# Sliding-window attention gated by a SiLU feed-forward layer: where Wo's halves are stored, how early raw weights are fetched, and where the last transposes stand

## The chip, the cores and the metric

The kernel runs on one core of one Trainium2 chip. The core has a matrix engine (TensorE, "PE" in the profile, with its weight loads as "PEld"), three engines for elementwise work (VectorE "DVE", ScalarE "ACT", GpSimd "POOL"), a queue engine (SyncE, "SP") and 16 DMA engines. Each engine works through its own list of instructions in order and waits on semaphores for the others. The metric is the time of one execution in device microseconds; lower is better.

## The reference

All arrays are float32; x is 2048 x 640 (S x D). With xn = layernorm(x), without learned scale:

```
q, k, v = split(xn @ wqkv) into 32 heads of 20
logits[s, w] = q[s] . k[s - 2 w] / sqrt(20)       w = 0..7, positions below 0 masked
o[s] = sum over w of softmax(logits[s])[w] * v[s - 2 w]
s_out = o @ wo                                      wo: 640 x 640
h = silu(xn @ w1);  g = silu(h @ w2)                w1: 640 x 1536, w2: 1536 x 640
out = x + s_out * g
```

## The kernel before, in words

**Precision.** PE multiplies in a float32 format of reduced precision (fp32r). To keep float32's, each operand is split in two halves: the high half is a rounded copy, the low half what is left. A product takes three passes: high x high, low x high, high x low. For a weight chunk the split is one ACT copy (L407) and one subtraction (L413, on DVE but for the first few). A chunk that has been split once can be kept in DRAM as a pair of halves (`half_...`, stored by L418) and loaded back by POOL's queue in one transfer (L399) with no work on ACT or DVE. A pair has 640 KB, the raw chunk 320 KB.

**Groups and stages.** The 2048 positions are worked on in four groups of 512: two halves of the sequence, each cut into even and odd positions, so that the window of stride 2 has stride 1 inside a group. In a group, `qkv_phase` computes q, k and v in four quarters of the heads, each from five weight chunks; evacuations go to ACT, and `halo` copies the seven earlier rows that a window needs from one partition to the next (L509 on SP). `scores` and `values` do the attention on DVE, in broadcast multiplies and reductions; this is long and runs behind the matmuls, into the next stage. `ffn_phase` then does, for f = 0 to 12, the first product of w1 chunk f (15 matmuls of 512 columns, L888 to L890) and the second product of w2 chunk f - 1 (12 pairs of 384 and 256 columns, L743 and L745).

**Wo, one group late.** The attention output of group g is transposed and split during the q/k/v stage of group g + 1 (`o_chunk`, through L475), and its product with Wo (`wo_phase`, five chunks of 12 pairs, L743/L745 again) stands in `ffn_phase` of group g + 1 behind the first product of f = 0. So Wo is used four times: in groups 1, 2 and 3, and at the end (`wo_last`) for group 3's own output. Group 3's output is transposed inside group 3's feed-forward stage, the last two chunks of it by `o_rest` (L590). `wo_rest` finishes group 2's rows there: four adds on DVE (L804) and four stores of output rows (L806).

**Units.** The list `units` names every use of a weight chunk in order of use: 44 in group 0 (20 of q/k/v, 24 of w1 and w2), 49 in each later group, 5 at the end. In group 1 the Wo chunks are units 65 to 69, in group 2 114 to 118, in group 3 163 to 167, at the end 191 to 195. Unit i lives in slot i mod 7 of the ring `WR`; `w_load` is called for the next unit when one has been used (`w_done`), so a load can run seven units ahead. `what` says how each use gets its halves: "split" (raw load, split, nothing kept), "store" (raw load, split, halves kept in DRAM), "load" (halves from DRAM). `store_at` is the use at which the halves are stored: the first one, but the second for the q/k/v chunks with odd c.

**Raw chunks.** The raw chunks (`fresh` lists their units) are fetched by SP (`raw_load`, L379/L381) into buffers: in group 0 into several tiles, later into the two tiles `XR` in turn. The fetch of the chunk two further on in `fresh` is asked for at each split. `XR` also takes the rows of x that `wo_phase` adds to the result (L788, the add on POOL L789, the store L791).

**The order of the work.** Nothing is issued as the program text runs. Each operation is added to `Weave` with an engine, a modelled duration, what it reads and writes, and a priority. `Weave.order` then plays the program through with these durations (a DMA model of one shared pipe of 310 KB per us plus a landing time of 1.9 us) and always starts the operation that can start first, the lower priority number among those ready. PE's operations keep the order in which they were added. The order so found is emitted, each engine's list in order; on the chip the engines keep it even where the real times differ from the modelled ones. ACT's weight copies have the lowest priority, raw loads on SP `clock + 5`, halo copies `clock`, stores of halves `due + 25`.

Of the kernel before, what the change touches and what calls it, by code (L numbers as in the profile page):

```python
# [15 lines left out]
S, D, F, H, DH = 2048, 640, 1536, 32, 20  # L16
W = 8
DC, FC = D // P, F // P
# [9 lines left out]
EPS = 1e-5  # L28
CA, CB = 384, 256
RING = 7  # L30
WARM, WARM2 = 20, 3
HOLD = 3.4
LO = 10
# [142 lines left out]
def local_attention_silu_ffn(ctx: ExitStack, tc: tile.TileContext, x, wqkv, wo, w1, w2, out):  # L176
# [126 lines left out]

    def store_at(u):

        return 1 + (u[0] == "q" and u[2] % 2)

    first_q = NQ * DC

# [27 lines left out]
    def raw_load(k):  # L337
# [43 lines left out]
                nc.sync.dma_start(to, by)  # L381
        dma(go, [], kr, n * P * 4, 1 + k if k < 2 * DC else clock[0] + 5, (0.62 if k < 2 * DC else 0.45) * (1 + len(more)))

    def w_load():
        i = loaded[0]
        if i >= len(units):
            return
        loaded[0] += 1
        u, s = units[i], i % RING
        n = width(i)  # L390
        r = WR[s]
        at = start(i)
        both = r.rearrange("p (s d) -> p s d", s=2)[:, :, at:at + n]
        whi, wlo = both[:, 0], both[:, 1]
        kh, kl = ("wh", s), ("wl", s)
        due = clock[0]
        if what[i] == "load":
            src = halves[u]
            add("POOL", 1.0, lambda: nc.gpsimd.dma_start(both, src), [("half", u), ("half", u, "more")], [kh, kl], due + 10,  # L399
                nbytes=2 * n * P * 4)  # L400
            return
        k = fresh.index(i)
        if not k:
            raw_load(0)
            rawn[0] = 1
        raw, kr = raws.pop(i)
        act(n, lambda: nc.scalar.activation(whi, raw, AF.Copy), kr + [("sd", 0)] * (k < 2), [kh], 1000 + due)  # L407
        pool_does = k < LO and k not in ON_DVE
        eng, cost, by = ("POOL", po(n), nc.gpsimd) if pool_does else ("DVE", dv(n), nc.vector)
        parts = HALVES if pool_does and k < DC else 1  # L410
        for j in range(parts):
            cs = slice(j * n // parts, (j + 1) * n // parts)
            add(eng, po(n // parts) if pool_does else cost, lambda cs=cs: by.tensor_tensor(  # L413
                out=wlo[:, cs], in0=raw[:, cs], in1=whi[:, cs].bitcast(F32), op=OP.subtract), [kh] + kr,
                [kl if j == parts - 1 else kl + (j,)], due if pool_does else LOW_AT if k < LO else 50, lock=True)
        if what[i] == "store":
            def keep(to, a, b, key):
                dma(lambda: nc.sync.dma_start(to, both[:, :, a:b].bitcast(F32)), [kh, kl], [key], 2 * (b - a) * P * 4,  # L418
                    due + 25)
            wide = width(len(units) - 1 - units[::-1].index(u))  # L420
            kept = dram.tile([P, 2, wide], F32, name="half_" + "_".join(map(str, u)))
            halves[u] = kept
            past = n - wide if u[0] == "q" and u[1] == NQ - 1 else 0
            keep(kept[:, :, :n - past], past, n, ("half", u))
            for k in range(past // MORE):
                v = ("q", k, u[2])
                keep(halves[v][:, :, 3 * CQ:], k * MORE, (k + 1) * MORE, ("half", v, "more"))
        while rawn[0] <= (min(k + 6, early - 1) if k < early - 2 else k + 2):
            raw_load(rawn[0])
            rawn[0] += 1  # L430

    def w_next(*want):

# [322 lines left out]
    def gkeys(ts, cs):  # L756
        return [("g", t, cs.start) for t in range(ts.start, ts.stop)]
# [34 lines left out]

    rest = []

    def wo_rest(g):

        done = [("o", NQ - 1, t) for t in (0, 2)]
        for t, xr, kx in rest:
            if t >= 2:
                dma(lambda t=t, xr=xr: nc.sync.dma_start(xr, rows(xg, g)[:, t, :]), done, [(kx[0], t)] if t > 2 else kx,  # L800
                    P * D * 4, clock[0])
        for t, xr, kx in rest:
            kx = [(kx[0], t)] if t > 2 else kx
            dve(D, lambda t=t, xr=xr: nc.vector.tensor_tensor(out=xr, in0=xr, in1=G[:, t, :], op=OP.add),  # L804
                done + gkeys(slice(t, t + 1), slice(0, CA)) + gkeys(slice(t, t + 1), slice(CA, D)), kx, 600, lock=True)
            dma(lambda t=t, xr=xr: nc.sync.dma_start(rows(og, g)[:, t, :], xr), kx, [], P * D * 4, clock[0] + 5)  # L806

    def wo_last(g, i):
# [52 lines left out]
    def ffn_phase(g, i, ix, io):  # L861
        nxt = g + 1 if g + 1 < NG else None
        ps = prev = None
        for f in range(FC + 1):
            if nxt is not None and f == 0:
                load_x(nxt, 0, 2)
                load_x(nxt, 2, 2)
                for t in range(T):
                    ln_stats(t)
                ln_rstd(0, T)  # L870
                for t in range(T):
                    ln_apply(t)
            if nxt is not None and XT_AT <= f < XT_AT + DC:
                split_t(XIN, [("xin", t) for t in range(T)], f - XT_AT, ix, (TH, TL))
            if nxt is None and f in OL_AT:
                o_chunk(g, OL_AT[f], io)
            if nxt is None and f in REST_AT:
                o_rest(g, REST_AT[f], io)
            cur = None
            if f < FC:  # L880
                wh, wl, kh, kl = w_next("w1", f)
                h, kp = rot()
                s = f % 2

                def first(cs=range(DC), wh=wh, wl=wl, h=h):
                    for c in cs:
                        cs = tsl(c)
                        nc.tensor.matmul(h, wh[:, cs], TH[i][:, c, :], start=c == 0, stop=False)  # L888
                        nc.tensor.matmul(h, wh[:, cs], TL[i][:, c, :], start=False, stop=False)  # L889
                        nc.tensor.matmul(h, wl[:, cs], TH[i][:, c, :], start=False, stop=c == DC - 1)  # L890
                if nxt is None and f == FC - 1:
                    pe(12 * mm(TOK), lambda first=first: first(range(4)), t_keys(i, range(DC)) + [kh, kl], [kp])
                    o_rest(g, (2, 3), io)
                    wo_rest(g - 1)
                    pe(3 * mm(TOK), lambda first=first: first(range(4, DC)), t_keys(i, range(DC)) + [kh, kl], [kp])
                else:
                    pe(15 * mm(TOK), first, t_keys(i, range(DC)) + [kh, kl], [kp])
                w_done()
                sf, sh, sl = SF[s], SH[s], SL[s]
                act(TOK, lambda sh=sh, h=h: nc.scalar.activation(sh, h, AF.Silu), [kp], [("sh", s)], 0, "silu")  # L900
                act(TOK, lambda sf=sf, h=h: nc.scalar.activation(sf, h, AF.Silu), [kp], [("sf", s)], 0, "silu")
                dve(TOK, lambda sf=sf, sh=sh, sl=sl: nc.vector.tensor_tensor(
                    out=sl, in0=sf, in1=sh.bitcast(F32), op=OP.subtract), [("sf", s), ("sh", s)], [("sl", s)], 0, lock=True)
                cur = sh, sl, ("sh", s), ("sl", s)
                if g and f == 0:
                    wo_phase(g - 1, io)
            if f:
                sh, sl, ksh, ksl = prev
                if ps is None:
                    ps = tm_banks()  # L910
                a, b = ps
                wh, wl, kh, kl = w_next("w2", f - 1)
                for t in range(T):
                    def big(t=t, f=f, wh=wh, wl=wl, sh=sh):
                        tm_mm(ps, t, sh[:, tsl(t)], wh, f == 1, False)
                        tm_mm(ps, t, sh[:, tsl(t)], wl, False, False)

                    def small(t=t, f=f, wh=wh, sl=sl):
                        tm_mm(ps, t, sl[:, tsl(t)], wh, False, f == FC)
                    ko = [a[t][1], b[t // 2][1]]  # L920
                    pe(2 * TM, big, [ksh, kh, kl], ko)
                    if f == FC:
                        pe(TM, small, [ksl, kh], ko)
                    else:
                        late.append((TM, small, [ksl, kh], ko))
                for args in late:
                    pe(*args)
                late.clear()
                w_done()
            prev = cur  # L930
        for p, kp, ts, cs in tm_views(ps):
            n = (ts.stop - ts.start) * (cs.stop - cs.start)
            act(n, lambda p=p, ts=ts, cs=cs: nc.scalar.activation(G[:, ts, cs], p, AF.Silu), [kp], gkeys(ts, cs), 0, "silu")
# [41 lines left out]
```

## Time and profile before

| | us |
|---|---|
| median of 3 runs (lowest, highest) | 643.68 (641.07, 643.97) |
| the profiled execution: its own time | 643.34 |
| its span, first to last instruction | 641.5 |
| PE busy | 632.7 |
| DVE busy | 537.5 |
| ACT busy | 210.2 |
| POOL busy | 117.7 |

The mean granted clock of PE was 0.995 of full speed. The DMA queues moved 162.45 MB, 82.58 of them on POOL's queue (q0) and 78.88 on SP's (q1). Group 0 takes about the first 148 us, groups 1, 2 and 3 about 160 us each, and `wo_last` the last 18 or so.

Lines such as "DVE pr L532 <- DMA kv<-kv: 36.8, 2, 30.2" say: DVE, at line 532, which writes pr, waited for the transfer named; 36.8 us in total, twice, 30.2 the longest. In a timeline a row has its start, its duration, the engine, the line, the operation, output and input tiles and their shapes, and in brackets how long the engine was idle before it and what released it.

### The profile page before, as it was taken

Reading aid. Unit: us, or ns where it says so; the run is one execution under the profiler, and the core shown is the slowest. Engines: PE = TensorE matmul, PEld = TensorE weight load, DVE = VectorE, ACT = ScalarE, POOL = GpSimd, SP = SyncE. Lnnn points to the kernel's source line nnn. Section 1 sums busy time; section 2 is a strip of 40 time slices with the busy share of each in tenths; the row PEclk is TensorE's granted clock in tenths of the full one; section 3 lists DMA queues with packets and bytes.
Section 4 is the critical chain, followed back from the end, with each engine's and each line's share of the span. In section 5 each row is a group of like instructions: output and inputs, shape, how many; then the busy total and the mean of one; then the engine's idle time right before and its main releaser. Section 6 shows DMA issues by size and latency. Waiting matters only on the chain.

```text
span 641.5 us, 9077 instructions
## 1 busy us (share of the span) xinstructions
PE 632.7 (99%) x3495; PEld 572.1 (89%) x3495; DVE 537.5 (84%) x543; ACT 210.2 (33%) x439; POOL 117.7 (18%) x164
## 2 busy tenths in 40 slices
PE   7999999999999899999999999999999999999997
PEld 6888899998889898999888999999988999899997
DVE  6699899999989778989959998999504999999824
ACT  4535463443435013142423302323313231223220
POOL 4410000001110134111222115211222211111100
PEclk8999999999999999999999999999999999999999
DMA  9899999877998988756699998855769998566652
GB/s 284 286 305 299 308 385 403 346 217 218 315 281 263 327 298 257 250 173 214 189 257 230 316 261 286 275 179 172 231 174 278 245 315 261 177 196 190 187 198 82
DMA packets 77499, 162.45 MB, mean 253 GB/s; under 512 B 9248, under 2 KB 38912, under 8 KB 77456
## 3 DMA queue, kind: packets, MB, share of 16 engines
q0 software_dynamic: 26672, 82.58, 43.9%
q1 hardware_dynamic: 50240, 78.88, 39.3%
q8 instruction: 27, 0.44, 0.3%
q10 hardware_dynamic: 544, 0.41, 0.2%
q14 instruction: 16, 0.13, 0.1%
HBM read 109.55 MB, written 34.16 MB: 224 GB/s over the span
## 4 chain that ended last, share of the span: by engine, by line
PE 93%; DVE 3%; DMA 2%; issue 1%; ACT 0%; DVEq 0%; ACTq 0%
PE acc L743 21%; PE acc L745 14%; PE acc L709 9%; PE acc L707 9%; PE acc L708 9%; PE rot L890 8%; PE rot L889 8%; PE rot L888 8%; PE rot L475 2%; DMA xr<-in_A_wo_dram 2%; PE acc L650 2%; DVE w L413 1%; DMA xin<-in_A_x_dram 1%; DVE l L535 0%; DVE st L615 0%
## 5 line engine op out<-in xcount | busy, mean ns | idle before, releaser
L532 DVE TENSOR_TENSOR pr<-q,kv 128x2560 f32<-128x2560 f32 x32 | 90.3, 2821 | 36.9 <-DMA kv<-kv 36.8
L743 PE MATMUL acc<-w,sh 128*128 128x384 f32 x384 | 113.6, 335 | 0.0
L707 PE MATMUL acc<-w,th 128*128 128x512 f32 (+2 forms) x300 | 113.3, 378 | 0.0
L709 PE MATMUL acc<-w,th 128*128 128x512 f32 (+2 forms) x300 | 112.9, 376 | 0.0
L708 PE MATMUL acc<-w,tl 128*128 128x512 f32 (+2 forms) x300 | 112.8, 376 | 0.0
L745 PE MATMUL acc<-w,sh 128*128 128x256 f32 x384 | 107.1, 279 | 0.0
L888 PE MATMUL rot<-th,w 128*128 128x512 f32 x240 | 95.8, 399 | 0.0
L890 PE MATMUL rot<-th,w 128*128 128x512 f32 x240 | 94.0, 392 | 0.0
L889 PE MATMUL rot<-tl,w 128*128 128x512 f32 x240 | 93.9, 391 | 0.0
L564 DVE TENSOR_TENSOR pr<-e,kv 128x2560 f32<-128x2560 f32 x32 | 90.3, 2823 | 0.7
L535 DVE TENSOR_REDUCE l<-pr 128x128 f32<-128x2560 f32 x32 | 90.1, 2815 | 0.4
L399 POOL DMA_DIRECT2D w<-half_q x52 | 37.4, 719 | 238.9 <-DVE pr L569 93.2
L569 DVE TENSOR_TENSOR pr<-pr 128x1280 f32<-128x1280 f32 x64 | 76.0, 1188 | 1.0
L399 POOL DMA_DIRECT2D w<-half_w x72 | 38.6, 537 | 198.7 <-PE acc L745 88.7
L745 PEld LDWEIGHTS acc<-w,sh 128*128 128x128 f32 x384 | 72.3, 188 | 1.6
L743 PEld LDWEIGHTS acc<-w,sh 128*128 128x128 f32 x384 | 72.1, 188 | 1.7
L900 ACT ACTIVATE sh<-rot 128x512 fp32r<-128x512 f32 x48 | 28.7, 599 | 126.1 <-PE rot L890 121.4
L709 PEld LDWEIGHTS acc<-w,th 128*128 128x128 f32 x300 | 56.3, 188 | 8.8
L708 PEld LDWEIGHTS acc<-w,tl 128*128 128x128 f32 x300 | 56.3, 188 | 8.6
L707 PEld LDWEIGHTS acc<-w,th 128*128 128x128 f32 x300 | 56.3, 188 | 8.5
L743 PE MATMUL acc<-w,sl 128*128 128x384 f32 x192 | 57.9, 333 | 0.0
L491 ACT ACTIVATE kv<-acc 128x320 f32<-128x320 f32 x64 | 28.3, 442 | 84.8 <-PE acc L709 82.2
(94 smaller groups left out, 1003.7 us busy)
## 6 DMA issues: line engine op xcount, KB each, us to landing
w<-half_w POOLq DMA_DIRECT2D x72, 640.0 KB, 5.3
w<-half_q POOLq DMA_DIRECT2D x39, 512.0 KB, 4.1
half_w<-w SPq DMA_DIRECT2D x24, 640.0 KB
w<-half_wo POOLq DMA_DIRECT2D x15, 640.0 KB, 9.0
kv<-kv SPq DMA_DIRECT2D x16, 560.0 KB
kv<-kv SPq DMA_DIRECT2D x16, 420.0 KB
gate<-in_B_w_dram SPq DMA_DIRECT2D x16, 320.0 KB
w<-half_q POOLq DMA_DIRECT2D x13, 384.0 KB, 4.7
```

The lines of the kernel that those rows point to most:

```text
L399: add("POOL", 1.0, lambda: nc.gpsimd.dma_start(both, src), [("half", u), ("half", u, "more")], [kh, kl], due + 10, nbytes=2 * n * P * 4)
L532: dve(2560, lambda t=t: nc.vector.tensor_tensor(out=PR, in0=win(qq[:, t:t + 2, :], W, 0), in1=win(kv[:, 0, t:t + 2, :], W, CQ), op=OP.mult ...
L535: dve(2560, lambda t=t: nc.vector.tensor_reduce(out=l[:, t:t + 2].rearrange("p t w h -> p (t w h)"), in_=PR.rearrange("p t w (h d) -> p (t ...
L564: dve(2560, lambda t=t, v=v: nc.vector.tensor_tensor(out=PR.rearrange("p t w (h d) -> p t (w h) d", d=DH), in0=e[:, t:t + 2].rearrange("p ...
L707: nc.tensor.matmul(o, hi, wh, start=c == 0, stop=False)
L708: nc.tensor.matmul(o, lo, wh, start=False, stop=False)
L709: nc.tensor.matmul(o, hi, wl, start=False, stop=c == DC - 1)
L743: nc.tensor.matmul(a[t][0][:, :CA], st, w[:, :CA], start=first, stop=last)
L745: nc.tensor.matmul(b[t // 2][0][:, h * CB:(h + 1) * CB], st, w[:, CA:], start=first and h == 0, stop=last, skip_group_check=True)
L888: nc.tensor.matmul(h, wh[:, cs], TH[i][:, c, :], start=c == 0, stop=False)
L889: nc.tensor.matmul(h, wh[:, cs], TL[i][:, c, :], start=False, stop=False)
L890: nc.tensor.matmul(h, wl[:, cs], TH[i][:, c, :], start=False, stop=c == DC - 1)
```

## The change

Three parts.

1. `store_at` gives Wo's chunks 2 instead of 1. Units 65 to 69 are now "split", 114 to 118 "store", the later ones "load" as before.
2. The loop that asks for raw chunks becomes the function `raws_due`, which also runs when a unit is loaded as halves, and stops at a raw chunk whose unit lies more than `RAW_AHEAD` = 10 units ahead of the one now being loaded.
3. In the last group, the first product of f = 11 is cut after the second of its five chunks instead of the fourth; the transposes of `o_rest` and the work of `wo_rest` stand at the cut. The four adds of `wo_rest` also read all tiles of the halves of group 3's attention output, so that they come after the last of these are written.

```diff
+RAW_AHEAD = 10
...
-        return 1 + (u[0] == "q" and u[2] % 2)
+        return 1 + (u[0] == "wo" or u[0] == "q" and u[2] % 2)
...
+    def raws_due(i, k):
+
+        while rawn[0] <= (min(k + 6, early - 1) if k < early - 2 else k + 2):
+            if rawn[0] < len(fresh) and fresh[rawn[0]] > i + RAW_AHEAD:
+                break
+            raw_load(rawn[0])
+            rawn[0] += 1
+
     def w_load():
...
             add("POOL", 1.0, lambda: nc.gpsimd.dma_start(both, src), [("half", u), ("half", u, "more")], [kh, kl], due + 10,
                 nbytes=2 * n * P * 4)
+            raws_due(i, sum(j < i for j in fresh) - 1)
             return
...
-        while rawn[0] <= (min(k + 6, early - 1) if k < early - 2 else k + 2):
-            raw_load(rawn[0])
-            rawn[0] += 1
+        raws_due(i, k)
...
-    def wo_rest(g):
+    def wo_rest(g, i):
...
-                done + gkeys(slice(t, t + 1), slice(0, CA)) + gkeys(slice(t, t + 1), slice(CA, D)), kx, 600, lock=True)
+                done + t_keys(i, range(DC)) + gkeys(slice(t, t + 1), slice(0, CA)) + gkeys(slice(t, t + 1), slice(CA, D)), kx, 600, lock=True)
...
-                    pe(12 * mm(TOK), lambda first=first: first(range(4)), t_keys(i, range(DC)) + [kh, kl], [kp])
+                    pe(6 * mm(TOK), lambda first=first: first(range(2)), t_keys(i, range(DC)) + [kh, kl], [kp])
                     o_rest(g, (2, 3), io)
-                    wo_rest(g - 1)
-                    pe(3 * mm(TOK), lambda first=first: first(range(4, DC)), t_keys(i, range(DC)) + [kh, kl], [kp])
+                    wo_rest(g - 1, io)
+                    pe(9 * mm(TOK), lambda first=first: first(range(2, DC)), t_keys(i, range(DC)) + [kh, kl], [kp])
```

## The prediction

> **What bounds the kernel now.** I read the page first, then the table of waits, then the PE timeline around the waits it names. "Unit 69" is the 70th entry of the list of weight units, and so on.
>
> ```profile
> span 641.5 us, 9077 instructions
> ...
> PE 632.7 (99%) x3495; PEld 572.1 (89%) x3495; DVE 537.5 (84%) x543; ACT 210.2 (33%) x439; POOL 117.7 (18%) x164
> ...
> PE 93%; DVE 3%; DMA 2%; issue 1%; ACT 0%; DVEq 0%; ACTq 0%
> ```
>
> TensorE sets the time: 632.7 of 641.5 us busy. The change removes no matmul, so it can only touch PE's waits, or matmuls that ran slowly while counted as busy. The waits (who waited for whom: total, times, longest):
>
> ```profile
> DVE pr L532 <- DMA kv<-kv: 36.8, 2, 30.2
> ...
> ACT w L407 <- DMA xr<-in_A_wo_dram: 12.9, 1, 12.9
> ...
> PE acc L743 <- ACT w L407: 1.5, 1, 1.5
> ...
> PE acc L743 <- DVE w L413: 0.3, 1, 0.3
> ```
>
> PE waited 1.8 us behind one raw chunk of Wo: its load is late, ACT's copy (the high half) waits 12.9 us for it, the DVE subtraction (the low half) follows, PE last. The real loss is larger. The PE timeline (start, duration) and the stretches around the wait (length; busy per engine; PEclk, DMA share, GB/s):
>
> ```profile
> 213.80 0.33 PE L743 MATMUL acc<-w,th 128*128 128x384 f32 x1
> ...
> 219.25 0.33 PE L743 MATMUL acc<-w,tl 128*128 128x384 f32 x1
> ...
> 226.91 0.40 PE L888 MATMUL rot<-th,w 128*128 128x512 f32 x1
> ```
>
> ```profile
> 219.50:222.00 2.50, 0.76 (x4) 0.30 (x2) 0.84 (x2) 0.74 (x1) 0.00 (x0) 1.00 0.99 380
> ...
> 223.00:226.00 3.00, 3.00 (x13) 3.00 (x13) 3.00 (x4) 0.00 (x0) 0.54 (x2) 0.50 1.04 328
> 226.00:227.00 1.00, 1.00 (x8) 1.00 (x8) 0.72 (x3) 0.00 (x0) 0.61 (x1) 0.98 0.91 287
> ```
>
> From 213.80 to 219.25 there are 19 pairs (a 384- and a 256-column matmul): 5.45 / 19 = 0.287 us a pair. Unit 69, the fifth Wo chunk, would start at 219.25 + 0.287 = 219.54, and its 12 pairs (four token tiles, three passes) would end at 219.54 + 3.44 = 222.98. The next product started at 226.91, so the loss is **3.93 us**: 1.8 of waiting, and 2.15 because the granted clock was 0.50 from 223 to 226. That is 0.6% of the run, and the one place in groups 1 to 3 where PE waits.
>
> **Why the chunk was late.** SP's issues around it, with the copies, the subtractions and the weight load that compete:
>
> ```profile
> 197.56 0.36 SPq L379 DMA_DIRECT2D xr<-in_A_wo_dram  x1
> 198.02 0.37 SPq L418 DMA_DIRECT2D half_wo<-w  x1
> ...
> 198.95 1.27 SPq L418 DMA_DIRECT2D half_wo<-w  x1
> 203.48 4.26 SPq L509 DMA_DIRECT2D kv<-kv  x4
> ...
> 208.31 0.36 SPq L379 DMA_DIRECT2D xr<-in_A_wo_dram  x1
> 208.72 1.57 SPq L418 DMA_DIRECT2D half_wo<-w  x2
> ```
>
> ```profile
> 203.75 1.38 ACT L407 ACTIVATE w<-xr 128x640 fp32r<-128x640 f32 x2
> ...
> 220.38 0.74 ACT L407 ACTIVATE w<-xr 128x640 fp32r<-128x640 f32 x1 [12.85 <-DMA xr<-in_A_wo_dram]
> ```
>
> ```profile
> 204.93 1.55 DVE L413 TENSOR_TENSOR w<-xr,w 128x640 fp32r<-128x640 f32 x2
> ```
>
> ```profile
> 202.35 0.54 POOL L399 DMA_DIRECT2D w<-half_w  x1 [13.46 <-PE acc L709]
> ```
>
> The last raw chunk is issued at 208.31 and used at 220.38, 12.07 us later. In the queues (q1 is SP's, q0 POOL's; packets, MB, share of 16 engines), first 200 to 204 us, then 204 to 214:
>
> ```profile
> q1 hardware_dynamic: 469, 1.66, 102.4%
> ```
>
> ```profile
> q1 hardware_dynamic: 604, 1.31, 53.7%
> q0 software_dynamic: 277, 1.27, 51.5%
> ```
>
> Between 200 and 204, q1 moves 1.66 MB, mainly the two stores, and POOL's load of 202.35 moves nothing. That load then shares 204 to 214 with the halo (the four L509 copies, about 1.1 MB) that stands ahead of the raw chunk. The two stores of 208.72 follow.
>
> **The change, part by part.**
>
> *Stores move from group 1 to group 2.* Five stores of 640 KB (3.28 MB) leave 198 to 222 us. Without the first two the load of 202.35 moves at once: 0.66 MB at 1.66/4 = 0.415 MB/us is 1.6 us, done near 204.5, and the halo then shares q1's time with two loads instead of three. The halo plus chunk (1.1 + 0.33 MB), at the 0.26 MB/us that both queues moved in 204 to 214 with a load of 0.66 MB between, needs 2.1/0.26 = 8 us from 204: landing near 212, latest perhaps 216. PE needs the high half at 219.54, so the load must land by 219.54 - 0.74 = 218.8. I take the whole 3.93 us as gained; bounds 0 and -3.93.
>
> *Group 2 uses raw chunks.* The five POOL loads of the halves go; five raw loads (1.64 MB), five copies, five subtractions and five stores come. The group before:
>
> ```profile
> 350.55 0.54 POOL L399 DMA_DIRECT2D w<-half_wo  x1 [2.15 <-PE acc L709]
> ...
> 361.85 0.53 POOL L399 DMA_DIRECT2D w<-half_w  x1 [1.55 <-PE acc L709]
> ```
>
> ```profile
> 362.98 3.09 SPq L509 DMA_DIRECT2D kv<-kv  x4
> ```
>
> ```profile
> 364.84 0.68 DVE L480 TENSOR_TENSOR tl<-rot,th 128x512 fp32r<-128x512 f32 x1
> ```
>
> ```profile
> 365.26 0.34 PE L743 MATMUL acc<-w,th 128*128 128x384 f32 x1
> ...
> 382.48 0.40 PE L888 MATMUL rot<-th,w 128*128 128x512 f32 x1
> ```
>
> Work: 5 x 0.69 = 3.5 us on ACT (1.38 / 2 each), idle two thirds of the time, and 5 x 0.78 = 3.9 us on DVE (1.55 / 2 each). DVE is late here, but its 30.2 us wait (the row of L532 above, at the start of group 3) takes up such a delay. Without that cover 3.9 us would be the price. SP's ten more issues of about 0.4 us here stand in a queue that is mostly idle; POOL loses five of 0.54. Cost 0.
>
> The wait is the point. Group 2's Wo product starts at 365.26, group 1's at 219.54 - 48 x 0.287 = 205.76: the same pattern 159.5 us later, with the halo at 362.98 (203.48 + 159.5) and the weight load at 361.85 (202.35 + 159.5). So group 2 will have what group 1 had: two raw loads, two stores, halo, fifth raw chunk (unit 118), two stores. What differs is the issue. The chunk's buffer is free when the third chunk's subtraction is done; that fits behind L480 (ends 365.52), so 366.3, and SP's halo issues end at 366.07 (3.09 us here, 4.26 in group 1). Issue near 366.4 is 206.9 on group 1's clock, 1.4 us earlier. With the same 12.07 us it lands at 378.5. PE needs the high half at 365.26 + 48 x 0.287 = 379.04 and gets it at 379.25; it needs the low half one pair later, 379.33, and gets it near 380.05. Wait: 0.2 + 0.5 = **0.7 us**, too short, I judge, to lower the clock. Upper end by the nearest row: the landing hangs on the queue, not the issue, so 220.38 + 159.5 = 379.9, and the loss repeats at 3.93. Lower end 0: 0.7 us less would do, and halo copies that are issued in 3.09 us instead of 4.26 may leave the queue sooner by that much. I take 0.7, nearer to the row of the issue than to that of the landing, since the chunk goes straight behind the halo in both.
>
> The row for the clock: 1.8 us of idling within 2.3 us was followed by 3 us at 0.50. The Trainium skill (TensorE: Matmul & The Clock Gate, Part 1, What's actually happening) has the clock fall after an idle window of about 3.4 us. The trace had it fall after less. By that rule a wait of up to 1.8 us in group 2 would cost the wait alone, and the rival that repeats the loss would give an estimated 641.5; by the row it gives 643.7.
>
> *Raw loads at most ten units ahead.* Units 114 and 115 (Wo in group 2) are asked for when units 104 and 105 are loaded, not already at 68 and 69, where they would hold both XR buffers through group 1's output rows. Group 0 and 1 keep their order, since a raw load there comes at most six units ahead. Cost 0; the cover is the two-buffer ring, idle between the groups.
>
> *Last transposes after the second chunk.*
>
> ```profile
> 610.19 0.39 PE L888 MATMUL rot<-th,w 128*128 128x512 f32 x1
> ...
> 611.56 0.60 PE L590 MATMUL rot<-ident,o 128*128 128x128 f32 x4
> ...
> 612.70 0.34 PE L743 MATMUL acc<-w,sh 128*128 128x384 f32 x1
> ```
>
> ```profile
> 606.89 0.49 DVE L572 TENSOR_TENSOR o<-pr 128x320 f32<-128x320 f32 x1
> ...
> 612.27 1.56 DVE L804 TENSOR_TENSOR pr<-pr,gate 128x640 f32<-128x640 f32 x2 [1.95 <-DMA pr<-in_A_x_dram]
> ...
> 614.35 0.68 DVE L902 TENSOR_TENSOR sl<-sf,sh 128x512 fp32r<-128x512 f32 x1
> ```
>
> ```profile
> 633.38 1.93 PE L743 MATMUL acc<-w,th 128*128 128x384 f32 x10
> ```
>
> The four transposes move from 611.56 to 610.19 (six matmuls in). Their input is written at 607.38, so 2.8 us of cover stay where 4.2 were. All four output adds (L804, 1.56 / 2 = 0.78 each) now follow the last subtraction of the attention output, which ends some 1.9 us after the transposes start (0.60, then a copy and a subtraction of about 0.65): 612.1. If all four stand ahead of L902 on DVE, its end moves to 612.1 + 3.1 + 0.68 = 615.9; PE first uses it 14 pairs after 612.70, at 616.9. PE is dense here and 1.0 us of cover stays, so 0; were the cover gone, PE would wait for the adds, up to 3.1 us. Their output stores have until the end of the run, 25 us. One oddity: from 612.70 to 633.38 the 69 pairs take 20.68 / 69 = 0.300 us each, 0.013 more than in group 1, 0.9 us in all, and it begins at these transposes. Where they stand may decide it: bounds -0.9 and 0; I take 0, for nothing names the cause.
>
> **Sum.** 643.34 (the profiled execution: span 641.5 and 1.8 around it) - 3.93 + 0.7 + 0 = 640.1. The median of the runs is 0.34 above the profiled one, so **640.4**, 0.5% faster. Its own range: 639.7 (no wait) to 641.2 (1.5 us, clock kept).
>
> **Rivals.**
>
> *The loss moves to group 2.* For it: the halo and the weight load come at the same places of the pattern to 0.01 us, so the queues fill alike. Against: the earlier issue. Gain 3.93, loss 3.93: 643.7.
>
> *Slower: the fifth raw chunk lands behind all four stores.* The planner's order on SP follows modelled times; if the stores of the third and fourth chunk are put ahead of unit 118's load, 1.31 MB at 0.415 MB/us delay it by 3.2 us, to 383.1. High and low half follow 0.74 and 0.78 later, so PE waits about 5 us and loses 2.15 at half clock: 7.1. Net +3.2: 646.9. Against: in group 1 the load came first, 208.31 before 208.72. From a landing of 379.9 on the change loses.
>
> *The stores were not the cause.* q1 had served the first two before the halo was issued, and the last two come after the chunk. If the halo alone held it up, group 1 keeps its loss: 643.7 or more. Against: q0's load pushed into the halo's time. The Trainium skill (DMA: Bandwidth & Descriptors, Queues, rings and completion order) says descriptors of one queue are consumed in ring order; by that rule stores issued after the chunk cannot hold it up, which speaks for this rival.
>
> *Clean, and the tail loses its extra 0.013 us a pair.* 643.7 - 3.93 - 0.9 = 638.8.
>
> **Chances.** Forecast 0.43; loss moves 0.24; slower 0.18; not the cause 0.05; clean with the quick tail 0.10. What a measurement of this kernel can tell from no change is about 0.5%, 3.2 us, so faster means under 640.5: 0.30 of the forecast's 0.43, and the 0.10, is 0.40. Within: 0.13 + 0.24 + 0.05 = 0.42. Slower: 0.18. The range 638.8 to 646.9 takes in half of the slower case and of the quick tail.
>
> **What would show it.** Group 1: no PE wait on ACT w L407 near 220, granted clock 1.00 there, next product near 223. Group 2: the copy of the fifth chunk starting near 378.5 less 3.9 (all is that much earlier), PEclk near 1.00 in its Wo stretch; 0.50 shows the first rival, a landing some 3 us later the second. Tail: transposes six matmuls into the last first product; the spacing of pairs after them. I am wrong if PE gains a wait in another place, since the planner recomputes every engine's order.

## The result, and the profile after

The changed kernel takes 641.59 us (median of 22 runs, 638.67 to 644.2), the kernel before 642.38 (22 runs, 638.33 to 647.88). The ratio is 0.9989, with a 95% interval of 0.9970 to 1.0008: no difference that these runs can tell. The profiled execution after has a span of 639.3 us, 2.2 less than the one before, but single executions of either kernel differ by more than that.

The page after, lines as before:

```profile
span 639.3 us, 9112 instructions
...
PE 630.3 (99%) x3495; PEld 569.4 (89%) x3495; DVE 542.5 (85%) x548; ACT 213.5 (33%) x444; POOL 113.0 (18%) x159
...
PE 88%; DVE 6%; DMA 4%; issue 1%; ACT 1%; SPq 0%; DVEq 0%; ACTq 0%
```

DVE has five instructions and 5.0 us more, ACT five and 3.3 us, POOL five fewer. Two waits of PE have the same cause and nearly the same length as before (L751, L417 and L423 are the old L743, L407 and L413):

```profile
PE acc L751 <- ACT w L417: 1.4, 1, 1.4
PE acc L751 <- DVE w L423: 0.3, 1, 0.3
```

They stand in another group. The PE timeline after, first and last row of group 1's Wo product, then of group 2's with the two waits:

```profile
205.71 0.34 PE L751 MATMUL acc<-w,th 128*128 128x384 f32 x1
...
222.92 0.40 PE L896 MATMUL rot<-th,w 128*128 128x512 f32 x1
```

```profile
361.31 0.34 PE L751 MATMUL acc<-w,th 128*128 128x384 f32 x1
...
376.61 0.45 PE L751 MATMUL acc<-w,th 128*128 128x384 f32 x1 [1.36 <-ACT w L417]
...
377.47 0.44 PE L751 MATMUL acc<-w,th 128*128 128x384 f32 x1 [0.29 <-DVE w L423]
...
380.73 0.40 PE L896 MATMUL rot<-th,w 128*128 128x512 f32 x1
```

Undisturbed, a Wo product takes 17.21 us (60 pairs of 0.287). Group 1's now does: 222.92 - 205.71 = 17.21, where it took 21.15. Group 2's takes 19.42, 2.21 too long. (The waits' rows add up to 1.65 only, since idle time counts from the modelled end of the matmul before, which overlaps.) What made the chunk late in group 2 is in the rows of SP and ACT after (first SP in group 2, then the halo and the fifth raw chunk in group 1, then ACT's copy of that chunk in groups 1 and 2):

```profile
353.63 0.36 SPq L428 DMA_DIRECT2D half_wo<-w  x1
...
354.63 1.21 SPq L428 DMA_DIRECT2D half_wo<-w  x1
359.03 4.15 SPq L517 DMA_DIRECT2D kv<-kv  x4
363.67 0.34 SPq L380 DMA_DIRECT2D xr<-in_A_wo_dram  x1
364.18 1.59 SPq L428 DMA_DIRECT2D half_wo<-w  x2
```

```profile
203.42 4.16 SPq L517 DMA_DIRECT2D kv<-kv  x4
...
208.17 0.95 SPq L380 DMA_DIRECT2D xr<-in_A_wo_dram  x1
```

```profile
214.95 0.74 ACT L417 ACTIVATE w<-xr 128x640 fp32r<-128x640 f32 x1 [7.48 <-DMA xr<-in_A_wo_dram]
```

```profile
375.82 0.74 ACT L417 ACTIVATE w<-xr 128x640 fp32r<-128x640 f32 x1 [11.88 <-DMA xr<-in_A_wo_dram]
```

It is group 1's old picture: two stores, the halo, the fifth raw chunk, two stores. The chunk is used 375.82 - 363.67 = 12.15 us after its issue. In group 1, now without stores, 214.95 - 208.17 = 6.8 us.

The tail changed too. PE after, around the moved transposes (L598) and the last pairs:

```profile
608.22 0.40 PE L898 MATMUL rot<-th,w 128*128 128x512 f32 x1
608.63 0.66 PE L598 MATMUL rot<-ident,o 128*128 128x128 f32 x4
...
611.21 0.34 PE L751 MATMUL acc<-w,sh 128*128 128x384 f32 x1
...
631.00 1.89 PE L751 MATMUL acc<-w,th 128*128 128x384 f32 x10
```

The same 69 pairs take 19.79 us, 0.287 each, where they took 20.68. The transposes start 0.41 us after the matmul before them, 0.18 more than its 0.23: they need the PSUM bank that the transposes before them filled, and DVE's subtraction from it ended at 608.58. In all the tail wins 0.89 and loses 0.25.

So in this pair of executions -3.94 in group 1, +2.21 in group 2 and -0.64 in the tail make -2.4 us; the spans differ by 2.2. The other 0.2 us stands at the very end: from the last 384-column matmul to the end of the span it is 5.68 us before and 5.86 after.

### The profile page after: what moved, and what is told of

It is laid out like the page before. It is cut to its first block, busy times and chain, and to the rows that moved or that the text cites. A ratio compares the mean times of both kernels' runs of the same rounds, so it can differ in the third digit from the quotient of the medians.

```text
span 639.3 us, 9112 instructions
## 1 busy us (share of the span) xinstructions
PE 630.3 (99%) x3495; PEld 569.4 (89%) x3495; DVE 542.5 (85%) x548; ACT 213.5 (33%) x444; POOL 113.0 (18%) x159
## 4 chain that ended last, share of the span: by engine, by line
PE 88%; DVE 6%; DMA 4%; issue 1%; ACT 1%; SPq 0%; DVEq 0%; ACTq 0%
PE acc L751 20%; PE acc L753 14%; PE rot L898 8%; PE rot L896 8%; PE rot L897 8%; PE acc L716 8%; PE acc L715 8%; PE acc L717 8%; PE rot L483 2%; DMA xr<-in_A_wo_dram 2%; DVE pr L540 2%; PE acc L658 2%; DMA kv<-kv 2%; DVE l L543 1%; DMA xin<-in_A_x_dram 0%
## 5 line engine op out<-in xcount | busy, mean ns | idle before, releaser
L751 PE MATMUL acc<-w,sh 128*128 128x384 f32 x384 | 113.4, 334 | 0.0
L577 DVE TENSOR_TENSOR pr<-pr 128x1280 f32<-128x1280 f32 x64 | 73.8, 1153 | 1.0
L751 PEld LDWEIGHTS acc<-w,sh 128*128 128x128 f32 x384 | 72.1, 188 | 1.7
L751 PE MATMUL acc<-w,sl 128*128 128x384 f32 x192 | 57.8, 332 | 0.0
```

What stands on the lines that cost most here:

```text
L751: nc.tensor.matmul(a[t][0][:, :CA], st, w[:, :CA], start=first, stop=last)
```

## The experiments

Theory: the loss moved to group 2, because the fifth raw chunk stands behind the halo, and the halo is pushed back by the stores ahead of it; whether the clock then falls differs by execution. Rivals: the change does gain, and the clock falls in group 1 only; or the full queues delay whatever comes next.

**Both kernels again, and each with the other's tail** (one profile each). a1 and a2 are the two kernels as they are. a3 is the changed kernel with the third part undone:

```diff
-                    pe(6 * mm(TOK), lambda first=first: first(range(2)), ...)
+                    pe(12 * mm(TOK), lambda first=first: first(range(4)), ...)
                     o_rest(g, (2, 3), io)
                     wo_rest(g - 1, io)
-                    pe(9 * mm(TOK), lambda first=first: first(range(2, DC)), ...)
+                    pe(3 * mm(TOK), lambda first=first: first(range(4, DC)), ...)
...
-                done + t_keys(i, range(DC)) + gkeys(...) + ...
+                done + gkeys(...) + ...
```

and a4 the kernel before with these lines the other way round.

> The kernel before, profiled once more. Theory (the loss moves, the clock falls by chance): PE again waits some 1.8 us (1.5 and 0.3) for the fifth Wo chunk near 220 us of the span, and the granted clock after it is 0.50 or 1.00 as it happens: group 1's Wo product is lengthened by 3.9 us with the fall, by 2.2 without. Rival (the clock falls at this place every time): 0.50 after the wait again, 3.9 us. For the tail: if the place of the last transposes sets the spacing, the last pairs take 0.300 us again; if it varies by execution, it may be 0.287.

> The changed kernel, profiled once more. Theory (the loss moves, the clock falls by chance): no wait in group 1, a wait of some 1.7 us for the fifth chunk in group 2 near 376 us, and the clock after it 1.00 or 0.50 as it happens; span 639.3 without the fall, about 641 with it. Rival (no fall of the clock in group 2): 1.00 every time, span 639.3. Tail: pairs at 0.287 us if the place of the transposes sets it.

> The change without its third part: the transposes back behind the fourth chunk, the adds not held back. If the place of the transposes sets the spacing, the pairs after them take 0.300 us and the tail is about 0.9 us longer than with the change, less the 0.25 us that the earlier transposes cost the last first product: net 0.6 longer. If it varies by execution, 0.287 is as likely. Groups 1 and 2 as with the change.

> The kernel before with the third part alone. If the place of the transposes sets the spacing, 0.287 us a pair, tail 0.6 us shorter in all than before (0.9 gained, 0.25 lost at the transposes). If it varies, 0.300 is as likely. Group 1 as before: waits of 1.5 and 0.3 us for the fifth chunk.

a1's waits in group 1, and the clock behind them (the last three columns are PEclk, DMA share, GB/s):

```profile
219.89 0.44 PE L743 MATMUL acc<-w,th 128*128 128x384 f32 x1 [1.18 <-ACT w L407]
...
220.75 0.44 PE L743 MATMUL acc<-w,th 128*128 128x384 f32 x1 [0.31 <-DVE w L413]
```

```profile
222.00:224.00 2.00, 2.00 (x16) 2.00 (x15) 2.00 (x3) 0.00 (x0) 0.53 (x1) 1.00 1.01 310
```

a2's, in group 2:

```profile
361.43 0.34 PE L751 MATMUL acc<-w,th 128*128 128x384 f32 x1
...
377.90 0.44 PE L751 MATMUL acc<-w,th 128*128 128x384 f32 x1 [2.54 <-ACT w L417]
...
383.62 0.39 PE L896 MATMUL rot<-th,w 128*128 128x512 f32 x1
```

```profile
380.00:382.00 2.00, 2.00 (x9) 2.00 (x9) 2.00 (x2) 0.42 (x1) 0.53 (x1) 0.50 1.00 312
```

The same readings for all kernels in which the chunk came late, with b5 from below (excess: length of the Wo product less 17.21; waits: the two rows of ACT and DVE added; idle: PE's most idle time in one clock window, explained below; pairs: spacing of the last ones):

| execution | late in group | waits, us | idle, us | clock after | excess, us | pairs, us |
|---|---|---|---|---|---|---|
| before | 1 | 1.78 | 1.78 | 0.50 | 3.94 | 0.300 |
| a1 before again | 1 | 1.49 | 1.18 | 1.00 | 2.03 | 0.300 |
| a4 before, new tail | 1 | 1.75 | 1.37 | 1.00 | 2.31 | 0.287 |
| after | 2 | 1.65 | 0.93 | 1.00 | 2.21 | 0.287 |
| a2 after again | 2 | 2.84 | 1.83 | 0.50 | 4.98 | 0.287 |
| a3 after, old tail | 2 | 2.95 | 2.58 | 0.50 | 5.07 | 0.300 |
| b5 last two stores late | 2 | 2.51 | 2.34 | 0.50 | 4.50 | 0.287 |

No kernel has a loss in both groups. The rival by which the clock falls in group 1 only is out, and "by chance" needs a limit: the clock fell after all three waits of 2.5 us or more and after one of four between 1.5 and 1.8.

The traces' records of the granted clock say why. Within an execution every change of the clock stands a whole number of windows of 3.41 us from the first change, in all 13 traces (before: 4.18, 7.60, 11.01, 222.64 and 226.05 us), and a fall in mid-run lasts one window. Counted over all these windows, the clock fell at the end of every one in which PE's rows leave 1.75 us or more idle, and of none with 1.51 or less; in between, one of 1.52 fell and two of 1.63 and 1.64 did not. So it matters where the wait lies: the changed kernel's profile had a window's edge at 376.18, inside the wait, which cut it into 0.93 and 0.73 us, and the clock held; a2 had 1.83 us in one window, and it fell.

The same records show a fall that no Wo chunk causes: in six of the 13 profiles (before, after, a2, a3, b1, c1) the clock is at 0.50 for one window between 7.5 and 12.9 us, at the start of group 0. These six reach group 1's Wo product at 205.7 to 206.7 us, the other seven at 204.5 to 205.4. Both profiles of the result have this fall, so it does not touch their difference. One fall brings the mean clock of an execution to about 0.997: 11 of the changed kernel's 22 runs have that, with a median of 642.83 us, and the other 11 have 640.61.

The mean excess is 2.8 us in the three executions with the stores in group 1 and 4.2 in the four with an excess in group 2 (4.1 without b5). With 0.64 won in the tail, that would make the change slower by some 0.8 us, where the runs have it faster by 0.8; so few executions say no more than that gain and loss are of one size. The tail follows the transposes' place in every execution.

**A buffer of its own for the fifth chunk**, in the changed kernel (b1) and in the kernel before (b2); twelve executions of each. The fetch is tied to a halo copy of the group's first quarter, so that it comes in the right group.

```diff
-    XR = tiles("xr", 2, [P, D])
+    XR = tiles("xr", 3, [P, D])
...
-            s = k % 2
+            s = 2 if u == ("wo", DC - 1) else k % 2
...
-        dma(go, [], kr, ...)
+        dma(go, [("halo", 0, 1, 0)] if u == ("wo", DC - 1) else [], kr, ...)
```

> The changed kernel with a buffer of its own for the fifth raw Wo chunk, fetched a few tens of us before its use instead of behind the halo. Theory (the late fifth chunk is the whole loss in group 2): no PE wait and no slow clock in groups 1 to 3; 2.2 us under the changed kernel where its clock held and 3.9 where it fell, so about 2 to 3 us under it in the median. Rival (the full DMA queues hold up whatever comes next): another chunk or a load of halves is late, PE waits again, no gain.

> The kernel before with the same buffer: the stores stay in group 1. Theory (not the stores but the late place of the fifth chunk in the queue costs the time): no PE wait in group 1, about 2 to 3 us under the kernel before, as good as the changed kernel with the buffer to within 1 us. Rival (the stores themselves cost): group 1 keeps a wait of 1 us or more, on this chunk or another.

b1: 638.26 us against 641.29 of the kernel before, ratio 0.9953 (0.9938 to 0.9968). b2: 638.39, ratio 0.9953 (0.9936 to 0.9970). Neither has a PE wait in groups 1 to 3. In b2 three stores of halves even stand ahead of the halo, the fifth chunk is copied at 198.79, and group 1's Wo product takes 221.94 - 204.72 = 17.22:

```profile
197.93 2.82 SPq L418 DMA_DIRECT2D half_wo<-w  x2
202.55 4.60 SPq L509 DMA_DIRECT2D kv<-kv  x4
```

```profile
198.79 0.74 ACT L407 ACTIVATE w<-xr 128x640 fp32r<-128x640 f32 x1 [5.38 <-PE acc L708]
```

```profile
204.72 0.34 PE L743 MATMUL acc<-w,th 128*128 128x384 f32 x1
...
221.94 0.40 PE L888 MATMUL rot<-th,w 128*128 128x512 f32 x1
```

So the stores may stay where they are. Time was lost because the last of five raw chunks, with two buffers in turn, had to be asked for behind the halo. In these two profiles the full queues delay nothing else that PE waits for in groups 1 to 3.

**Which stores hold the chunk up.** b3 holds back the first two of group 2's stores until the fifth chunk has landed, b5 the third and the fourth. The core of b3, where last[0] is the fetch of the fifth raw chunk (b5 does the same for the chunks 2 and 3):

```diff
-            keep(kept[:, :, :n - past], past, n, ("half", u))
+            if u[0] == "wo" and u[1] < 2:
+                held.append(lambda: keep(kept, 0, n, ("half", u), last[0]))
+            else:
+                keep(kept[:, :, :n - past], past, n, ("half", u))
...
+        if u == ("wo", DC - 1) and what[i] == "store":
+            for f in held:
+                f()
```

> The changed kernel with the first two of group 2's five stores held back until the fifth raw chunk has landed. If they delay the chunk, by pushing POOL's load into the halo's time, the chunk lands some 5 us sooner (a latency of about 7 us as in group 1 of the changed kernel, where there are no stores) and PE doesn't wait in group 2: span 2.2 us shorter than with the change, 637. If only what follows the chunk matters, the latency stays near 12 us.

> The changed kernel with the third and fourth store, which follow the fifth raw chunk in the queue, held back until it has landed. If descriptors of a queue are served in order, these stores can't delay the chunk: latency stays near 12 us and PE waits 1.7 us. If they share the engines with it, the latency falls by up to 3 us (1.31 MB at 0.41 MB/us) and the wait goes.

b3, the halo, the fifth chunk's issue, its use, and a new wait of PE:

```profile
357.82 4.09 SPq L525 DMA_DIRECT2D kv<-kv  x4
363.16 0.33 SPq L382 DMA_DIRECT2D xr<-in_A_wo_dram  x1
```

```profile
370.40 0.74 ACT L422 ACTIVATE w<-xr 128x640 fp32r<-128x640 f32 x1 [7.67 <-DMA xr<-in_A_wo_dram]
```

```profile
384.93 0.50 PE L904 MATMUL rot<-th,w 128*128 128x512 f32 x1 [0.55 <-DMA w<-half_w]
```

b5:

```profile
363.29 0.34 SPq L382 DMA_DIRECT2D xr<-in_A_wo_dram  x1
```

```profile
375.98 0.74 ACT L422 ACTIVATE w<-xr 128x640 fp32r<-128x640 f32 x1 [12.86 <-DMA xr<-in_A_wo_dram]
```

Without the two stores ahead the chunk takes 7.2 us, without the two behind it 12.7. b3 also moves POOL's next load (365.23 in the changed kernel, 372.38 here) out of the chunk's time, so it is not clean by itself; but group 1 of the changed kernel, with no stores and POOL's loads in place, has 6.8 us, and b5, with the first two stores and the same loads, 12.7. The stores ahead are the cause; those behind the chunk don't matter. With b2 this says that the loss needs two things, a fetch that stands behind the halo and stores that stand ahead of it; without either there is no loss.

The single packets in the traces show how. A store's rows go as packets of 5120 bytes, the halo's and the raw chunk's are smaller. The two stores' 256 packets are not all moved when SP starts to issue the halo: 68 of them start later in the kernel before, where the last ends at 205.04, and 78 in group 2 of the changed kernel, where it ends at 360.79. POOL's load of halves, issued about 1 us before the halo, moves its first packet 1.7 to 2.1 us after its issue (before, after, b5), without the stores 1.25 us after it (group 1 of the changed kernel, b3). So when the halo's packets begin, a third of the load is still to come with the stores ahead (86 and 87 of 128 packets moved), and under a tenth without (118 and 122). From issue to landing it takes 7.9 to 8.4 us with them and 4.5 to 4.6 without. It is pushed into the time of the halo and the chunk, as the prediction had it.

The time that SP takes to issue the halo does not come from these stores: 4.09 us in b3 and 4.16 in group 1 of the changed kernel without them, 4.15 with them. By the Trainium skill (DMA: Bandwidth & Descriptors, Queues, rings and completion order) each DMA engine consumes a queue's descriptors in ring order; b5 agrees, with 12.7 us without the two stores behind the chunk against 12.15 with them. b3's Wo product is clean (17.22), and it pays 0.55 us elsewhere: held stores hold their slots, and a load of w1's halves comes late.

**The best of both, and what the tail does.** c1 is b2 with the third part of the change. c2 and c3 cut the last first product after the third chunk and after the fifth:

```diff
-                    pe(6 * mm(TOK), lambda first=first: first(range(2)), ...)
+                    pe(9 * mm(TOK), lambda first=first: first(range(3)), ...)
...
-                    pe(9 * mm(TOK), lambda first=first: first(range(2, DC)), ...)
+                    pe(6 * mm(TOK), lambda first=first: first(range(3, DC)), ...)
```

> The kernel before with the own buffer for the fifth chunk and the third part of the change (transposes after the second chunk): Wo's halves still go to DRAM at the first use. If the two gains are independent: no wait in groups 1 to 3, last pairs at 0.287 us, span 0.65 us under that of the buffer alone (0.9 gained on the pairs, 0.25 lost at the transposes), about 3.5 us under the kernel before in the median: a ratio near 0.9945. Rival (moving the stores to group 2 has a worth of its own): slower than the changed kernel with the buffer.

> The same with the transposes after the third chunk: six matmuls of 512 columns stand between them and the pairs. Behind three such matmuls the pairs were slow to the end in every run, behind nine in none. Theory (the lead of PE's weight loads is lost at the transposes and comes back only while 512-column matmuls run): six may do, then 0.287 us and no wait of 0.2 us for the transposes' bank, 0.2 us under the cut after the second chunk. If six are too few: 0.300 us to the end, 0.9 us lost.

> The same with the transposes after all five chunks: no 512-column matmul between them and the pairs. By the same theory the pairs take 0.300 us or more to the end of the span. If instead a cut inside the product is what makes them slow, 0.287 us.

c1: 637.72 us against 641.44, ratio 0.9948 (0.9932 to 0.9964). c2: 637.71, ratio 0.9943 (0.9926 to 0.9961). No wait in groups 1 to 3 in either. c2 around its transposes:

```profile
606.08 0.39 PE L890 MATMUL rot<-th,w 128*128 128x512 f32 x1
606.31 0.60 PE L590 MATMUL rot<-ident,o 128*128 128x128 f32 x4
...
608.15 0.33 PE L743 MATMUL acc<-w,sh 128*128 128x384 f32 x1
608.32 0.28 PE L745 MATMUL acc<-w,sh 128*128 128x256 f32 x1
608.43 0.33 PE L743 MATMUL acc<-w,sh 128*128 128x384 f32 x1
```

c3:

```profile
607.36 0.60 PE L590 MATMUL rot<-ident,o 128*128 128x128 f32 x4
607.72 0.43 PE L743 MATMUL acc<-w,sh 128*128 128x384 f32 x1
...
608.39 0.34 PE L743 MATMUL acc<-w,sh 128*128 128x384 f32 x1
...
608.68 0.34 PE L743 MATMUL acc<-w,sh 128*128 128x384 f32 x1
```

Six matmuls are enough: c2's pairs take 0.287 us from the first, and its transposes come 0.23 us after the matmul before, without c1's wait. c3's take 0.300 to the end. A cut inside the product is therefore not what makes them slow; in all 13 profiles the slow pairs go with three such matmuls or fewer behind the transposes. Why, was not settled: that weight loads lose a lead there and win it back only under long matmuls fits all runs, but no row shows that lead.

c2 beats both kernels: its interval ends at 0.9961, that of the changed kernel begins at 0.9970, each against the kernel before. Among themselves the kernels with the third buffer, b1, b2, c1 and c2, can't be told apart: ratios of 0.9943 to 0.9953, with intervals that overlap. b1 has the moved stores and the quick tail, b2 has neither, and their medians are 0.13 us apart; so the tail's 0.64 us and the worth of moving the stores do not show in these medians, and the tail's gain is shown by the rows of the profiles alone. The runs also spread less: b2's twelve lie between 637.8 and 639.3 us, the 23 of the kernel before beside them between 638.4 and 644.3. Part of that is the late chunk and part the clock: none of b2's twelve has a mean clock under 0.999, while 12 of the 23 have 0.997 or less (median 642.66 us, the others 640.52, close to the changed kernel's 642.83 and 640.61). Two of b1's twelve and two of c1's six have 0.996 or 0.997 and take 1.7 and 1.2 us more in the median than the others, though neither profile shows a late chunk.

## Why the prediction was right or wrong

The range held the measured 641.59, but that says little for the reasoning: it is 8.1 us wide and takes in the first rival, and 1.3 us of the way down from 643.68 belongs to the kernel before itself, whose median of 22 runs is 642.38. A change of -3.3 us was forecast, and -0.8 measured. The forecast of 640.4, 0.5% faster, did not come true; the first rival did, the loss that moves to group 2, with part of the quick tail.

*Group 1.* Right as to the cause. The gain was taken as 3.93 us; group 1's Wo product got 3.94 shorter against the profiled execution. But without the stores POOL's load did not move at once: it landed at 206.86, not near 204.5, and the chunk at 214.95, not near 212, though still well before the 218.8 needed. The rival that denied that the stores were the cause is out; its premise, that both stores were served before the halo was issued, was a misreading of 1.66 MB in 200 to 204 us, since 0.35 MB of them moved after 203.48. That the size came out is luck: against a1 and a4 the gain is only 2.0 or 2.3, because the clock held there, so the sum took the dear execution for the rule. The split of the loss into 1.8 of waiting and 2.15 of slow clock was also off: the clock was at 0.50 for 3.41 us, which costs 1.7, and a4 lost 2.31 at full clock with waits of the same length. The waits' rows count some 0.5 us too little.

*Group 2, where the forecast failed.* The step was the issue "near 366.4", 1.4 us earlier than in group 1's pattern, from SP issuing the halo in 3.09 us. That row was of a group without raw Wo chunks. In the eight kernels with two buffers profiled here (before, after, a1 to a4, b3, b5) the four issues took 3.09 to 3.12 us in each of groups 1 to 3 without raw Wo chunks, and 4.0 to 4.7 in each with them, whether stores stood ahead or not. Which of the things that come with the raw chunks slows them stays open. With 4.15 us the chunk was issued at 363.67, which is 367.6 on the old clock, 3.95 us later. It landed 12.15 us after that, at 379.8 on the old clock, against 378.5 in the forecast and 379.9 at its upper end. The other half of the step was to add a fixed 12.07 us to the issue. The landing does not follow the issue from execution to execution: counted from the start of the Wo product, a1 issued the chunk 0.6 us later than the kernel before and used it 0.3 us earlier, and a2 issued it 0.1 us earlier than the changed kernel's first profile and used it 1.2 us later. The row of the landing was the better one to choose. The term of 0.7 us became a loss of 2.21 (rows of 1.65), and of 4.5 to 5.1 in three other executions, with rows of 2.5 to 2.95 and a fall of the clock.

*The clock.* The judgement that a short wait would keep it held for the profiled execution (1.65 us), but by the place of the wait in the clock's windows as much as by its length; it failed for the longer waits. The Trainium skill (TensorE: Matmul & The Clock Gate, Part 1, What's actually happening) has the clock fall after an idle window of about 3.4 us; here 1.52 us of idling in a window of 3.41 us was the least that a fall followed, and 1.75 us was always enough, so that the page's condition of a wholly idle window is not borne out.

*The transposes.* Costed at 0 with bounds of -0.9 and 0; they gave -0.89 and +0.25. That the spacing of the pairs hangs on their place was named as possible and is so in every run. The 0.25 was missed: the working looked at the data's readiness (2.8 us of cover), not at the PSUM bank that the second set of transposes shares with the first.

*The adds and the raw loads.* Right, at nothing. The planner put two of the four adds in front of the last silu subtraction, and PE did not wait. No raw load came early enough to hold XR through group 1's output rows, and DVE's extra 5.0 us made no PE wait.

*The slower rival* asked for all four stores ahead of the chunk. The order stayed: two ahead, two behind.

## What to carry to other kernels

A cost that comes from an order of transfers goes where the order goes: before moving stores out of a crowded stretch, lay the new stretch beside the old one, and take the landing of the old transfer, not its issue, as the forecast. Look for the transfer that PE waits for and ask why it stands so late in its queue; here a third buffer of 2.5 KB per partition did more than moving 3.28 MB of stores. And of a loss seen in one profile, profile the unchanged kernel again before counting on all of it; where the clock falls in some executions and not in others, compare those in which it fell equally often.

## What the runs showed of the hardware that was not expected

- Pairs of 384- and 256-column matmuls ran at 0.300 us instead of 0.287 for the last 20 us of the span, in all five kernels' executions with three 512-column matmuls or none between the last transposes and the pairs (before, a1, a3, b2, c3), and in none of the eight with six or nine (after, a2, a4, b1, b3, b5, c1, c2). The granted clock showed 1.00 in both.
- The granted clock changed only at the edges of windows of 3.41 us, whole numbers of windows apart within an execution. It fell to 0.50 for one window after each window with 1.75 us or more of idle PE, and after none with 1.51 us or less (13 traces). A wait of 1.65 us cut by an edge left it at 1.00; 1.78 us inside one window did not.
- Two stores of 640 KB on SP's queue delayed a load that POOL issued some 2 us behind the second of them: 7.9 to 8.4 us to its landing with them, 4.5 and 4.6 without. Its first packet moved 1.7 to 2.1 us after its issue with them, 1.25 without.
- Four halo copies took SP 3.09 us to issue in groups 2 and 3 of the kernel before, and 4.09 to 4.26 in groups with raw Wo chunks, with stores ahead of them (4.26 before, 4.15 after) and without (4.16 after, 4.09 in b3). What lengthens the issue is not known.
